# Turning the normalised rows on VectorE in place and storing them from ScalarE's queue

## The chip, the core and the metric

The kernel runs on one core of a Trainium2 chip. The metric is device time in microseconds of one execution, as the median of several runs. The profile comes from one profiled execution on that core.

## The reference

The inputs are q, k, v of shape (4, 8, 576, 64), two weight matrices for a first feed-forward stage and three with a gain for a second. All is float32.

```python
scores = scale * q @ k.T            # per batch and head, D = 64
scores = where(0 <= i - j < 128, scores - slope_h * |i - j|, -1e9)
x = softmax(scores) @ v             # to (2304 tokens, 512)
h = x @ w_in                        # 512 -> 2048
x = (h * clip(h + 3, 0, 6) / 6) @ w_out          # 2048 -> 512
xn = x / sqrt(mean(x * x) + 1e-6) * rms_g
g, val = xn @ w_gate, xn @ w_val    # 512 -> 1536 each
out = (g * sigmoid(g) * val) @ w_out2            # 1536 -> 512
```

## The kernel before

The 2304 tokens are 18 tiles of 128 rows, and three tiles are a block, so there are six blocks, 0 to 5. Every float32 operand of a large product is split into a high and a low float32r part, and each product is three matmuls (high by high, high by low, low by high).

*First feed-forward stage (L683 to L792).* The work runs in parts, in the order of `PARTS`: block 0 with its first 12 slices of the hidden dimension, block 1 with all 16, block 0 with its last 4, then blocks 2 to 5 with 16 each. A part is a loop over slices `m`, and one turn of this loop is called a step here. In a step TensorE computes `product1` (12 matmuls into the one PSUM bank `ps_h`), then pieces of the attention of a later block, then `product2` of the step before (three outputs `o0` to `o2` of three matmuls each). ScalarE and VectorE make the activation of the slice in turn: relu (ACT, L722), multiply (DVE, L723, the last reader of `ps_h`), high part (ACT, L728), low part (DVE, L734). The order of all instructions is written out by hand (`manual_schedule`), and every engine executes its own instructions in that order; the tile framework adds the waits between engines.

*Attention beside it.* For blocks 2 to 5 the attention of one pair of heads takes four steps, and its pieces return every four steps. In the step that begins a group of four (step 0 here), ACT first copies the transposed weights of the pair's first tile out of PSUM (`late`, L709 and L405) and TensorE then transposes those of the second tile into the same PSUM bank, `T` (L400). Step 1 transposes the third tile and splits the next q and k (L310 to L317); step 2 has the score matmuls (L348 or L357); step 3 has the products with v and, at its end, the transposes of the first tile. The last part (block 5) has no attention beside it.

*The rows between the stages (class `Norm`, L505).* When a block has its last `product2`, `Norm` copies the three outputs out of PSUM into three tiles `y` of 128 rows by 512 (L514 to L518). The pool holds three such tiles (`bufs=3`). Then, one tile per step, `square` sums the squares on ACT (L526) and POOL makes the inverse root (L527 to L529); `scale` multiplies the tile by it on DVE (L534); one such step later `back` transposes it with four TensorE transposes into one PSUM bank (L550); and `store`, at the start of the next step, copies this bank to SBUF on ACT (L539) and writes it to DRAM with one DMA of 256 KB from SP's queue (L541). From block 0's own `Norm` on, `back` and `scale` run only in steps 3 and 0 of each four (`go`, L701), and in every step in the last part. So a block's first and third tile are stored at the start of a step 1 and the second at the start of a step 0. Block 1's tiles are scaled and turned during the last part of block 0, in successive steps, and block 0's `Norm` is created, by L614 to L615, right after `back` has turned block 1's last tile; `store` of that tile comes in the next step.

*Second stage (L833 on).* It reads the turned rows of six tiles back as `x2raw` (`Inputs.load`, L634), with the 512 features on partitions in four chunks, scales them by the gain and multiplies them with the weights in seven products per slice (a seven-product scheme for 2x2 blocks). Block 5's `Norm` is finished here: `store` follows the first silu of a group (L945), `scale` the second sum (L946) and `back` the group's end (L957).

Of the kernel before, what the change touches and what calls it, by code (L numbers as in the profile page):

```python
# [10 lines left out]
F32 = mybir.dt.float32  # L11
# [9 lines left out]
P = 128  # L21
B, H, S, D = 4, 8, 576, 64
NT = B * S
NTILE = NT // P
DM = H * D
KC = DM // P
# [6 lines left out]
BLOCKS = [(i, 3) for i in range(0, NTILE, 3)]  # L33
# [28 lines left out]
PAIRS2 = NTILE // 6  # L62
# [11 lines left out]
def fused_kernel(ctx: ExitStack, tc: tile.TileContext, qd, kd, v, w1, w2, rms_g, out):  # L74
# [7 lines left out]
    vec, act, pool, pe, sp = nc.vector, nc.scalar, nc.gpsimd, nc.tensor, nc.sync  # L82
# [6 lines left out]
    dram = ctx.enter_context(tc.tile_pool(name="dram", bufs=1, space=DRAM))  # L89
    ps_out = ctx.enter_context(tc.tile_pool(name="ps_out", bufs=1, space=PSUM))  # L90
    ps_h = ctx.enter_context(tc.tile_pool(name="ps_h", bufs=1, space=PSUM))
    ps_a = ctx.enter_context(tc.tile_pool(name="ps_a", bufs=1, space=PSUM))


    ident = const.tile([P, P], F32, name="ident")
# [57 lines left out]
    class First:  # L153
# [3 lines left out]
        def __init__(self):  # L157
            self.raw = [room(k, [P, 2 * DM], U64, "wraw") for k in range(M1)]
            self.loaded, self.runs, self.tiles = 0, [], []

        def load(self, upto):
            while self.loaded < min(upto, M1):
                sp.dma_start(out=self.raw[self.loaded], in_=w1[self.loaded])
                self.loaded += 1
# [309 lines left out]
            x.scores()  # L474


    x2 = [dram.tile([P, KC, 6 * P], F32, tag=f"x2_{i}", name=f"x2_{i}") for i in range(PAIRS2)]

    def product1(ps, w, xs, n):

# [24 lines left out]
    class Norm:  # L505


        def __init__(self, b, outs, part=None):
            self.b, self.n, self.t = b, len(outs), 0
            self.y, self.ri, self.ps = [], {}, {}  # L510
            for i, o in enumerate(outs):
                y = ypool.tile([P, DM], F32, tag="y", name="y")
                if part:
                    vec.scalar_tensor_tensor(out=y, in0=o, scalar=1.0 / 6.0, in1=part[i], op0=ALU.mult, op1=ALU.add)  # L514
                elif i % 2:
                    act.activation(y, o, AF.Copy, scale=1.0 / 6.0)
                else:
                    vec.tensor_scalar(y, o, 1.0 / 6.0, None, ALU.mult)  # L518
                self.y.append(y)
            self.square(0)  # L520
# [13 lines left out]
                vec.tensor_scalar(self.y[t], self.y[t], self.ri[t], None, ALU.mult)  # L534

        def store(self):
            for k in list(self.ps):
                yt = ypool.tile([P, KC, P], F32, tag="yt", name="yt", bufs=1)
                act.copy(yt, self.ps.pop(k))  # L539
                i = BLOCKS[self.b][0] + k  # L540
                sp.dma_start(out=x2[i // 6][:, :, i % 6 * P : (i % 6 + 1) * P], in_=yt)  # L541

        def back(self):

            k = self.t - 1
            if 0 <= k < self.n:
                tag = "T" if self.b == len(BLOCKS) - 1 else f"S{k % 2}"
                ps = ps_a.tile([P, KC, P], F32, tag=tag, name="ps_x")
                for c in range(KC):
                    pe.transpose(ps[:, c], self.y[k][:, c * P : (c + 1) * P], ident)  # L550
                self.ps[k] = ps
            self.square(self.t + 1)
            self.t += 1
            return self.t <= self.n + 1
# [70 lines left out]
    class Inputs:  # L625
# [5 lines left out]

        def load(self):
            self.x = xpool.tile([P, KC, 6 * P], F32, tag="xs", name="x2raw")
            sp.dma_start(out=self.x, in_=x2[self.s])  # L634

        def block(self, r, c):
            return self.x[:, 2 * c : 2 * c + 2, r * self.n : (r + 1) * self.n]
# [45 lines left out]
    for p, (b, m0, m1) in enumerate(PARTS):  # L683
        n = BLOCKS[b][1]
        last = p == len(PARTS) - 1
        nq = n * P
        if p == 2:
            conv.close()
            ypool = ys.enter_context(tc.tile_pool(name="ypool", bufs=3, **OPEN))
        if last:  # L690
# [3 lines left out]
            ypool = p2.enter_context(tc.tile_pool(name="ypool2", bufs=3, **OPEN))  # L694
# [3 lines left out]
        for m in range(m0, m1):  # L698
# [13 lines left out]
            ps = ps_h.tile([P, 4 * P], F32, tag="h", name="ps_h")  # L712
# [8 lines left out]
            r = gpool.tile([P, 3 * P], F32, tag="t", name="t", bufs=1)  # L721
# [25 lines left out]
            if p == 0:  # L747
                k = m + 1
# [18 lines left out]
            if last:  # L767
# [6 lines left out]
                for x in early:  # L774
                    k = m - EARLY[x.m]
# [20 lines left out]
    n = 3 * P  # L796
# [109 lines left out]
    for m, x in parts.items():  # L906
        i = m - 2
# [32 lines left out]
    for i in range(M2 * PAIRS2):  # L940
        s, m = divmod(i, M2)
# [63 lines left out]
```

## Time and profile before

| what | value |
|---|---|
| time, median of 3 runs | 956.75 us (956.23 to 956.86) |
| span of the profiled execution, first to last instruction | 954.2 us |
| TensorE matmuls busy | 937.7 us, 98% |
| VectorE (DVE) busy | 640.5 us, 67% |
| ScalarE (ACT) busy | 454.2 us, 48% |
| GpSimd (POOL) busy | 186.3 us, 20% |
| DMA, all from SP's queue | 174.09 MB, 52.2% of 16 engines' time |
| TensorE clock granted, mean | 0.995 of full speed |

The page gives no time of the profiled execution besides its span; the median of the runs is 2.55 us longer than it. Instructions that issue DMAs aren't counted as busy: a row of such an instruction, marked SPq, gives the time for which SP was held by it.

### The profile page before, as it was taken

How to read it: one execution, taken by the hardware profiler on the slowest of the kernel's cores; microseconds unless marked ns; L12 is line 12 of the kernel's file. 1: busy time of each engine (PE TensorE's matmuls, PEld its weight loads, DVE VectorE, ACT ScalarE, POOL GpSimd, SP SyncE). 2: the span in 40 equal slices, each digit the busy share in tenths (PEclk: the TensorE clock that was granted, in tenths of full speed). 3: DMA queues.
4: the chain of work that ended last, by engine and by line, in shares of the span. 5: the costliest groups of instructions: out<-in, count | busy, mean ns of one | idle time of the engine just before them, and what ended most of it. 6: DMA issues, size and time to landing. Idle time of an engine off the chain costs nothing.

```text
span 954.2 us, 14654 instructions
## 1 busy us (share of the span) xinstructions
PE 937.7 (98%) x5336; PEld 832.9 (87%) x5336; DVE 640.5 (67%) x1336; ACT 454.2 (48%) x969; POOL 186.3 (20%) x327
## 2 busy tenths in 40 slices
PE   7899999999999999999999999999999999999998
PEld 4587888888888888888899999999999999999996
DVE  5788667555878777877467657777545577545555
ACT  6899566455666655655455453433131323231120
POOL 4333012332223332422124223310000000000000
PEclk8999999999999999999999999999999999999999
DMA  6555401113666555554355757866757555755521
GB/s 231 183 194 194 187 20 51 32 53 117 198 211 203 172 164 174 164 169 130 122 182 210 287 206 293 320 229 234 249 212 281 214 202 199 265 206 211 214 86 67
DMA packets 67432, 175.02 MB, mean 183 GB/s; under 512 B 5024, under 2 KB 41888, under 8 KB 62624
## 3 DMA queue, kind: packets, MB, share of 16 engines
q1 hardware_dynamic: 67360, 174.09, 52.2%
q8 instruction: 42, 0.69, 0.3%
q14 instruction: 30, 0.25, 0.1%
HBM read 130.03 MB, written 44.04 MB: 182 GB/s over the span
## 4 chain that ended last, share of the span: by engine, by line
PE 87%; DVE 6%; ACT 4%; issue 2%; POOL 1%; ACTq 0%; POOLq 0%; DVEq 0%
PE ps_o L497 19%; PE ps_h L484 18%; PE ps_y L892 15%; PE ps_o L845 10%; PE ps_S L845 8%; PE ps_A L845 6%; PE ps_h L845 4%; PE ps_av L418 2%; PE ps_t L400 2%; PE ps_s L357 1%; DVE wx L143 1%; PE ps_s L348 1%; ACT t L386 1%; ACT wx L136 1%; DVE t L371 1%
## 5 line engine op out<-in xcount | busy, mean ns | idle before, releaser
L497 PE MATMUL ps_o<-w,g 128*128 128x512 f32 x864 | 224.0, 402 | 2.1 <-DVE w L147 1.9
L484 PE MATMUL ps_h<-xs,w 128*128 128x384 f32 x1152 | 220.2, 339 | 0.0
L484 PEld LDWEIGHTS ps_h<-xs,w 128*128 128x128 f32 x1152 | 202.4, 188 | 5.8 <-issue 0.2
L497 PEld LDWEIGHTS ps_o<-w,g 128*128 128x128 f32 x864 | 156.2, 188 | 41.1 <-issue 6.3
L892 PE MATMUL ps_y<-wo,g 128*128 128x512 f32 x648 | 150.2, 390 | 0.5 <-DVE g L881 0.5
L892 PEld LDWEIGHTS ps_y<-wo,g 128*128 128x128 f32 x648 | 121.3, 188 | 25.1 <-DVE g L881 0.9
L723 DVE SCALAR_TENSOR_TENSOR t<-t,ps_h 128x384 f32<-128x384 f32 x96 | 53.2, 554 | 98.7 <-ACT t L722 98.6
L722 ACT ACTIVATE t<-ps_h,three 128x384 f32<-128x384 f32 x96 | 55.5, 578 | 84.1 <-PE ps_h L484 80.2
L899 DVE TENSOR_TENSOR y<-y,ps_y 128x512 f32<-128x512 f32 x90 | 61.7, 686 | 35.3 <-PE ps_y L892 35.0
L386 ACT ACTIVATE t<-t,m 128x128 f32<-128x128 f32 (+1 forms) x144 | 61.4, 428 | 29.4 <-DVE t L378 14.2
L728 ACT CAST g<-t 128x384 fp32r<-128x384 f32 x96 | 49.5, 516 | 47.5 <-DVE t L723 46.2
L734 DVE TENSOR_TENSOR g<-t,g 128x384 fp32r<-128x384 f32 x96 | 54.4, 567 | 23.3 <-ACT g L728 23.0
L868 ACT ACTIVATE r<-r 128x384 f32<-128x384 f32 x36 | 19.0, 527 | 105.6 <-DVE r L867 105.6
L845 PE MATMUL ps_o<-S,tw 128*128 128x384 f32 x336 | 66.2, 339 | 0.3 <-DVE t L865 0.3
L388 POOL TENSOR_SCALAR r<-den 128x2 f32<-128x2 f32 x72 | 27.4, 380 | 187.6 <-ACT t L386 186.0
L845 PEld LDWEIGHTS ps_o<-S,tw 128*128 128x128 f32 x336 | 59.3, 188 | 1.4 <-DVE u L856 0.8
L389 POOL TENSOR_TENSOR r<-r,minus 128x2 f32<-128x2 f32 x72 | 56.0, 778 | 6.0
L407 POOL TENSOR_SCALAR_AFFINE_SELECT pt<-pt 128x256 f32<-128x256 f32 x82 | 34.5, 421 | 107.5 <-ACT pt L405 104.5
L853 ACT COPY s<-ps_S 128x384 f32<-128x384 f32 x18 | 8.7, 481 | 86.9 <-PE ps_S L845 86.9
L371 DVE CUSTOM_DVE_ANT_0 t<-ps_s,rel 128x256 f32<-128x256 f32 (+2 forms) x128 | 45.2, 395 | 3.6 <-PE ps_s L357 3.6
L143 DVE SCALAR_TENSOR_TENSOR wx<-wx,wy 128x512 uint32<-128x512 uint32 (+1 forms) x52 | 44.2, 850 | 0.0
L136 ACT ACTIVATE wx<-wraw 128x512 f32<-128x512 f32 (+1 forms) x52 | 42.8, 824 | 0.0
(138 smaller groups left out, 1471.9 us busy)
## 6 DMA issues: line engine op xcount, KB each, us to landing
tw<-t SPq DMA_DIRECT2D x52, 896.0 KB, 6.3
wraw<-w SPq DMA_DIRECT2D x36, 512.0 KB, 4.1
wo<-w SPq DMA_DIRECT2D x18, 1024.0 KB, 4.9
wraw<-w SPq DMA_DIRECT2D x16, 1024.0 KB, 9.1
t<-th SPq DMA_DIRECT2D x12, 896.0 KB, 4.3
t<-tl SPq DMA_DIRECT2D x12, 896.0 KB, 4.3
b<-wx SPq DMA_DIRECT2D x24, 256.0 KB, 2.6
w<-w SPq DMA_DIRECT2D x12, 512.0 KB, 3.0
```

The source lines that it names most:

```text
L143: vec.scalar_tensor_tensor(out=xi, in0=xi, scalar=3, in1=y, op0=ALU.logical_shift_left, op1=ALU.bitwise_or)
L371: vec.tensor_tensor_reduce(out=self.t[:, a, c0:], in0=s[:, c0:], in1=(rel_split if self.i in SPLITS else rel)[:, c0:], scale=2.0 ** (-8.0 ...
L386: act.activation(p, p, AF.Exp, bias=self.m[:, a : a + 1], scale=-1.0, accum_out=self.den[:, a : a + 1])
L389: pool.tensor_tensor(self.r, self.r, minus, ALU.pow)
L484: pe.matmul(ps[:, : n * P], lhsT=w[:, a, c * P : (c + 1) * P], rhs=xs[c][:, b, : n * P], start=(k == 0), stop=(k == 3 * KC - 1),)
L497: pe.matmul(o, lhsT=g[:, a, i * P : (i + 1) * P], rhs=w[:, b], start=(m == first and a == 0 and b == 0), stop=(m == last and a == 1),)
L722: act.activation(r[:, :nq], ps[:, :nq], AF.Relu, bias=three)
L723: vec.scalar_tensor_tensor(out=r[:, :nq], in0=r[:, :nq], scalar=6.0, in1=ps[:, :nq], op0=ALU.min, op1=ALU.mult)
L734: vec.tensor_sub(g[:, 1, :nq], r[:, :nq], f32(g[:, 0, :nq]))
L845: pe.matmul(ps, lhsT=w[a][:, k, c * P : (c + 1) * P], rhs=x[:, b, c], start=(start and j == 0), stop=(j == 5), skip_group_check=True,)
L892: pe.matmul(ps, lhsT=gs[i + k][:, a, t // 3, t % 3 * P : (t % 3 + 1) * P], rhs=wo[i + k][:, b], start=(k == 0 and a == 0 and b == 0), stop ...
L899: vec.tensor_add(acc[t], acc[t], ps)
```

## The change

`back` no longer uses TensorE: it transposes the tile in place with one VectorE instruction, which turns each 32x32 block where it stands. `store` no longer copies anything: it issues four DMAs from ScalarE's own queue, one for each 32 partitions, and the DMA's destination puts the blocks where they belong. In such a quarter, partition r holds for each of 16 groups f of features the 32 tokens of feature 32 f + r, so one DMA has 32 x 16 = 512 runs of 32 floats, 128 bytes each. The DRAM tile `x2` becomes a plain matrix of 512 features by 768 tokens, and `load` reads it by rows of 768 floats into the same SBUF layout as before. The tile `y` is now read by the DMAs.

```diff
-    x2 = [dram.tile([P, KC, 6 * P], F32, tag=f"x2_{i}", name=f"x2_{i}") for i in range(PAIRS2)]
+    x2 = [dram.tile([DM, 6 * P], F32, tag=f"x2_{i}", name=f"x2_{i}") for i in range(PAIRS2)]
...
         def store(self):
-            for k in list(self.ps):
-                yt = ypool.tile([P, KC, P], F32, tag="yt", name="yt", bufs=1)
-                act.copy(yt, self.ps.pop(k))
-                i = BLOCKS[self.b][0] + k
-                sp.dma_start(out=x2[i // 6][:, :, i % 6 * P : (i % 6 + 1) * P], in_=yt)
+            for k in list(self.turned):
+                yt, i = self.turned.pop(k), BLOCKS[self.b][0] + k
+                for a in range(4):
+                    c0 = i % 6 * P + a * 32
+                    act.dma_start(
+                        out=x2[i // 6][:, c0 : c0 + 32].rearrange("(f r) s -> r f s", r=32),
+                        in_=yt[a * 32 : (a + 1) * 32].rearrange("r (f s) -> r f s", s=32),
+                    )
 
         def back(self):
 
             k = self.t - 1
             if 0 <= k < self.n:
-                tag = "T" if self.b == len(BLOCKS) - 1 else f"S{k % 2}"
-                ps = ps_a.tile([P, KC, P], F32, tag=tag, name="ps_x")
-                for c in range(KC):
-                    pe.transpose(ps[:, c], self.y[k][:, c * P : (c + 1) * P], ident)
-                self.ps[k] = ps
+                self.turned[k] = self.y[k]
+                vec.transpose(self.y[k], self.y[k])
             self.square(self.t + 1)
...
         def load(self):
             self.x = xpool.tile([P, KC, 6 * P], F32, tag="xs", name="x2raw")
-            sp.dma_start(out=self.x, in_=x2[self.s])
+            sp.dma_start(out=self.x, in_=x2[self.s].rearrange("(c p) n -> p c n", p=P))
```

## Rows read from the trace of the kernel before

**Rows 1.** The page, part 1: busy us, share of the span, instructions.

```profile
PE 937.7 (98%) x5336; PEld 832.9 (87%) x5336; DVE 640.5 (67%) x1336; ACT 454.2 (48%) x969; POOL 186.3 (20%) x327
```

**Rows 2.** Two stretches: length, busy us of PE, PEld, DVE, ACT, POOL, clock, DMA.

```profile
190.00:220.00 30.00, 30.00 (x186) 26.15 (x183) 16.17 (x49) 14.80 (x40) 9.09 (x21) 1.00 0.18 52
560.00:600.00 40.00, 39.73 (x214) 36.82 (x213) 25.79 (x36) 17.50 (x30) 11.62 (x13) 1.00 0.78 284
```

**Rows 3.** Chain of waits by windows: start us, us; first and last of 17.

```profile
207.36 0.44 PE ps_x L550 x4
...
588.11 0.44 PE ps_x L550 x4
```

**Rows 4.** Timeline, block 0's second tile (step 0): start us, us.

```profile
255.80 0.48 DVE L534 TENSOR_SCALAR y<-y,ri 128x512 f32<-128x512 f32 x1
256.46 0.38 ACT L405 COPY pt<-ps_t 128x256 f32<-128x256 f32 x1
258.08 0.38 PE L400 MATMUL ps_t<-ident,t 128*128 128x128 f32 x2
```

**Rows 5.** Timeline, block 0's first tile and the steps behind it.

```profile
239.44 0.48 DVE L534 TENSOR_SCALAR y<-y,ri 128x512 f32<-128x512 f32 x1
242.00 0.58 ACT L722 ACTIVATE t<-ps_h,three 128x384 f32<-128x384 f32 x1 [1.40 <-PE ps_h L484]
244.81 0.69 DVE L317 TENSOR_TENSOR ks<-kraw,ks 128x512 fp32r<-128x512 f32 x1
246.29 0.96 PE L348 MATMUL ps_s<-ks,qs 64*128 64x128 f32 x12
```

**Rows 6.** Lines 541 and 256 on SP, min/median/max ns; landing of 541's DMA.

```profile
L541 SPq DMA_DIRECT2D x<-yt x18: 512/548/621, 210.4 to 592.8; - x18
DMA to landing us min/median/max: 2.5/3.0/9.4
...
L256 SPq DMA_DIRECT2D t<-th x12: 319/320/383, 489.5 to 627.3; - x12
```

**Rows 7.** Timeline, block 2's second tile (block 3's has the same order).

```profile
340.22 0.58 ACT L539 COPY yt<-ps_x 128x512 f32<-128x512 f32 x1
340.68 0.38 ACT L405 COPY pt<-ps_t 128x256 f32<-128x256 f32 x1
```

**Rows 8.** Timeline, block 1's tiles and the start of block 0's `Norm`.

```profile
209.82 0.59 ACT L539 COPY yt<-ps_x 128x512 f32<-128x512 f32 x1
210.30 0.59 ACT L722 ACTIVATE t<-ps_h,three 128x384 f32<-128x384 f32 x1
213.38 0.48 DVE L534 TENSOR_SCALAR y<-y,ri 128x512 f32<-128x512 f32 x1
216.25 0.38 PE L400 MATMUL ps_t<-ident,t 128*128 128x128 f32 x2
218.73 1.88 DVE L514 SCALAR_TENSOR_TENSOR y<-ps_o,part 128x512 f32<-128x512 f32 x3
219.49 0.64 ACT L526 ACTIVATE junk<-y 128x512 f32<-128x512 f32 x1 [1.27 <-DVE y L514]
221.23 2.31 PE L497 MATMUL ps_o<-w,g 128*128 128x512 f32 x9
```

**Rows 9.** Timeline, block 4's tiles in the last part.

```profile
475.76 3.17 DVE L643 TENSOR_SCALAR x2raw<-x2raw,g_sb 128x768 f32<-128x768 f32 x4
480.02 2.35 PE L484 MATMUL ps_h<-xs,w 128*128 128x384 f32 x12
488.93 1.40 PE L484 MATMUL ps_h<-xs,w 128*128 128x384 f32 x7
```

**Rows 10.** The page, part 5: busy us, mean ns, idle before.

```profile
L723 DVE SCALAR_TENSOR_TENSOR t<-t,ps_h 128x384 f32<-128x384 f32 x96 | 53.2, 554 | 98.7 <-ACT t L722 98.6
L728 ACT CAST g<-t 128x384 fp32r<-128x384 f32 x96 | 49.5, 516 | 47.5 <-DVE t L723 46.2
L734 DVE TENSOR_TENSOR g<-t,g 128x384 fp32r<-128x384 f32 x96 | 54.4, 567 | 23.3 <-ACT g L728 23.0
```

More of the change, by code (lines that the diff above doesn't have):

```diff
@@ L509, in __init__ @@
             self.b, self.n, self.t = b, len(outs), 0
-            self.y, self.ri, self.ps = [], {}, {}
+            self.y, self.ri, self.turned = [], {}, {}
             for i, o in enumerate(outs):
```

## The prediction

> **What bounds the kernel now.** I read the page's busy shares first, then the chain of waits, then single stretches in order of time. TensorE is busy for 937.7 of 954.2 us [rows 1]; in the stretch of the first three stores it has no gap at all (30.00 of 30.00 us) [rows 2]. So a microsecond that leaves TensorE's order is worth a microsecond, and one in which TensorE has to wait costs one. The other engines matter only where TensorE waits for them, so what counts is how late ScalarE (ACT) and VectorE (DVE) may be in each single step. The span is 954.2 us and the median of the runs 956.75 us; I sum against the span and add the 2.55 us between them, as launch and end, unchanged.
>
> **What goes.** The four PE transposes of one tile stand on the chain with 0.44 us [rows 3]. The chain, window by window, holds 17 of the 18 groups (the other lies beside a longer chain of VectorE and ScalarE): 17 x 0.44 = 7.5 us is the most that TensorE can give back. The copy out of PSUM (0.58 us of ACT) and one DMA issue on SP go too. Nothing waits for that issue, except twice a next copy, so SP's relief is worth nothing.
>
> **What comes, per tile.** (1) One VectorE transpose of 128x512 f32, behind which all later DVE work of the step queues. The trace has none. The nearest rows are the in-place multiply of the same tile, 0.48 us [rows 4], and a two-input operation of the same size, 0.69 us [rows 5]. These are my bounds; I take 0.60, between them, since the transpose has one input like the first and its rate isn't shown. (2) Four DMA issues in ACT's own order. They wait for the transpose, and ACT executes in order, so the copy of attention weights (L405), the relu (L722) and the casts of the next step queue behind them. The trace has no issue on ACT; on SP the DMA with the same number of runs (512, then of 512 B, now of 128 B) takes 0.512 to 0.621 us, and the shortest issue of any kind 0.319 [rows 6]. I take 0.60 each with the gap to the next: 2.4 us per tile; the low end is 4 x 0.36 = 1.4, and for the high end I take 1.0 each, about twice SP's median, for four in a row.
>
> The Trainium skill ("Perfetto Trace Analysis", section DMA Instruction — HWDGE) says that the issuing sequencer is held from the end of its semaphore wait through a wait for the one descriptor generator until the descriptors are made. SP's rows agree in size; by that rule ACT would hold for all four.
>
> **Where it decides.** The steps of the first product have a rhythm of four. "Stored" is the start of the step after `back()`. I compare the start of the same instruction before and after; 0.44 us saved is inside each difference.
>
> *The second tile of blocks 0, 2, 3 (step 0 of four).* Here the copy of `late` weights follows the store on ACT, and TensorE's next transposes need the PSUM bank that this copy empties. In block 0 DVE's multiply ends at 256.28; transpose to 256.88; issues to 259.28; the 0.38 us copy to 259.66. TensorE's transposes started at 258.08 and now start at 259.7 [rows 4]: 1.6 us lost. In blocks 2 and 3 ACT first waits for a DVE conversion that now stands behind the new transpose; before, the copy of weights began 0.46 us after the PSUM copy and TensorE was already waiting for it [rows 7]. So +0.60 + 2.4 - 0.46 = 2.5 us lost each. Together 6.6 us.
>
> *The first and third tile of these blocks (step 1).* Multiply to 239.92, transpose to 240.52, issues to 242.92; the relu that began at 242.00 is 0.92 late. The chain relu, cast, split of k passes this on: the last DVE split ends at 246.4 and not 245.5, against a score matmul at 246.29 [rows 5]: 0.1 us lost. The two other first tiles come out near zero; for all three 0.4 us lost. For the third tiles, with no multiply ahead of the transpose, there is just room: 0.3 us gained each, 0.9 together.
>
> *Block 1.* Its first store comes where the copy began, 209.82; issues to 212.22, and the relu at 210.30 is 1.92 late. All DVE work behind it is, too: multiply to 215.78, transpose to 216.38, issues to 218.78, copy to 219.16, and TensorE's transposes slip from 216.25 to 219.2, by 2.95 us. Then a wait that was not there: block 0's three y tiles take the three buffers of tag `y`, and the third still holds block 1's last tile. Before, its PE transpose had read it. Now a DMA must, and `store()` issues that DMA one step later. Block 0's first write moves from 218.73 to 218.73 + 2.95 + 0.60 = 222.28; it lasts 0.63, the square on ACT some 0.8 to 223.7, the four issues to 226.1, the last of them starting at 225.5; landing takes a median of 3.0 us [rows 6], to 228.5; then the third write, to 229.2. TensorE's third output of the next second product needs that PSUM bank: the product would begin at 221.23 + 2.95 - 0.44 = 223.7 and reach it at 225.2. It waits 4.0 us and ends at 229.9, not 223.54 [rows 8]. Lost: 6.4 us.
>
> *Block 4 (no attention beside it).* DVE's four scalings begin at 475.76 and last 3.17; 0.60 ahead of them puts their end at 479.5, and after the 0.55 us of L723 the bank of `ps_h` is free at 480.1, where the first product began at 480.02 [rows 9, 10]: no gain. The next round is a ring: cast, subtract, multiply and transpose, 0.52 + 0.57 + 0.48 + 0.60, to 482.3; issues to 484.7; relu and L723, 0.58 + 0.55, to 485.8, with gaps 486.0, and only then may the first product start again. The last round has no multiply: 486.0 + 1.69 + 2.4 + 1.13 = 491.2 against 488.93 [rows 9, 10]. Lost: 2.3 us.
>
> *Block 5 (second product).* ACT is busy 17.50 of 40 us [rows 2]; it sits between long matmul groups, and the 2.4 us are hidden. Gain: 3 x 0.44 = 1.3 us. If that room were gone, as much as 2 us each would be lost.
>
> The load of x2 now reads 3 KB runs and not 12 KB; it is issued a step or more ahead, and I cost it at nothing. TensorE's clock shows 1.00, its higher level, in both stretches [rows 2]; waits of 2 to 4 us don't change that in my sum.
>
> **Sum:** -6.6 - 0.4 + 0.9 - 6.4 - 2.3 + 1.3 = -13.5, so 13.5 us lost. The span becomes 967.7, and with the 2.55 us outside it 970.2.
>
> The Trainium skill ("DMA: Bandwidth & Descriptors", Specifications) asks for at least 512 B per run for line rate and says that below it DMA reads, modifies and writes. No row here has data runs of 128 B. By it the landing in block 1 would be longer than 3.0 us: at twice that, 3 us more, 973.2.
>
> **Rivals.**
> *A cheap issue.* An issue on ACT costs what the simplest one costs on SP, 0.32 plus the gap, 1.4 us per tile [rows 6]. Then step 0 loses 0.7 in block 0 and 1.5 each in blocks 2 and 3; block 1 loses 3.7 (its slip is 0.9, the wait for the landing 3.3); block 4 loses 0.4; the first and third tiles gain 0.4 each (2.6), block 5 1.3. Net 3.9 lost: 960.7. Against it: the issue with the same count of runs never took under 0.512.
> *A crowded queue.* The four issues in a row can't hand over 2,048 runs as fast as SP hands over 512, and each takes 1.0 us. The 1.6 us more per tile pass on in about 12 of the 18 tiles, 19 us, and the landing is 3 us later: about 992. For it: landings of this DMA of up to 9.4 us [rows 6]. Against it: the median of 3.0.
> *Faster.* ACT gets past the issues nearly free, because the real cost is on the queue and not on the engine. From 0.60 to 0.36 per issue the loss falls by 9.6 us, so it turns into a gain below some 0.26 us each. At 0.1 the step-0 tiles lose about 1.5 in all, block 1 still loses 2.0 for its buffer, the rest gains 5: 955.2. If the buffer's wait were hidden too, 7.5 us: 949.2. Against it: no issue in the trace is below 0.319.
> *Block 1's buffer doesn't wait that long* (landing 2.0, or a free buffer): up to 4.0 less, 966.2. It lies within my range.
>
> **How the numbers follow.** Forecast 0.57 (its own range 964 to 978), cheap issue 0.18 (958 to 963), crowded queue 0.11, faster or even 0.14. What this kernel's measurement can tell from no change is about 0.2%, 1.9 us. Of the last case 0.09 is faster and 0.05 within that; of the cheap issue 0.02 comes within it as well. So faster 0.09, same 0.07, slower 0.84. The range is 956.5 to 984: it leaves out what is faster and the upper part of the crowded queue.
>
> **What would show it.** Four issues of 0.5 to 0.6 us in a row on ACT after each transpose; TensorE's transposes at step 0 (L400) idle until ACT's copy L405, some 2 us in three blocks and more in block 1; the third write of L514 waiting for a DMA near 223 us, and a gap of about 4 us in the second product there; TensorE's busy time down by about 10 us while the span grows. The forecast is wrong if the issues on ACT take under 0.3 us, if relu starts stay where they were, or if L514 doesn't wait.

## The result, and the profile after

The changed kernel takes 970.13 us (median; 966.86 to 973.09) against 956.49 us, a ratio of 1.0145, 95% interval 1.0130 to 1.0161. The forecast was 970.2. A second measurement of the same kernel, further down, gave 969.05 us and 1.0139 [1.0125, 1.0153]. The profiled execution is the quickest of the first four: 966.86 us, span 965.0, which is 10.8 us longer than the span before.

First the page of the changed kernel, parts 1, 3 and 4 (q1 is SP's queue, q10 ScalarE's):

```profile
PE 934.9 (97%) x5264; PEld 825.5 (86%) x5264; DVE 652.4 (68%) x1354; ACT 444.1 (46%) x951; POOL 183.5 (19%) x327
...
q1 hardware_dynamic: 59008, 169.37, 49.8%
q10 hardware_dynamic: 38016, 4.72, 3.2%
...
PE 73%; DVE 12%; ACT 7%; issue 3%; DMA 2%; ACTq 1%; POOL 1%; SPq 0%; POOLq 0%; DVEq 0%
```

TensorE has 72 instructions less than in [rows 1] and yet a longer span: 30.1 us of it are now idle, where it was 16.5. Its share of the chain that ended last is 73%, against 87% before.

The tile `y` in the changed kernel (min/median/max ns) answers to [rows 6]:

```profile
L541 ACTq DMA_DIRECT2D x<-y x72: 309/517/1874, 209.3 to 604.2; - x72
...
L551 DVE STREAM_TRANSPOSE y<-y x18: 698/704/708, 208.5 to 600.0; 128x512 f32<-128x512 f32 x18
...
DMA to landing us min/median/max: 1.8/2.3/12.9
```

So the transpose costs 0.70 us and an issue 0.52 us, and the data land in 2.3 us in the median, although the runs have 128 bytes. The windows of the changed kernel (columns as in [rows 2]):

```profile
190.00:220.00 30.00, 27.50 (x163) 23.57 (x160) 15.98 (x48) 13.19 (x37) 8.85 (x21) 0.96 0.28 65
218.50:222.00 3.50, 3.50 (x13) 2.84 (x12) 3.28 (x7) 1.32 (x4) 1.13 (x2) 0.65 0.94 302
258.00:266.00 8.00, 5.34 (x29) 4.48 (x29) 5.92 (x15) 3.56 (x8) 0.87 (x2) 1.00 0.93 269
266.00:270.00 4.00, 4.00 (x23) 3.67 (x22) 2.62 (x5) 0.94 (x3) 0.40 (x1) 1.00 0.76 145
```

The stretch of block 1's stores had no gap; now 2.5 of 30 us are idle. Behind that gap the clock shows 0.65: part of this stretch ran at half speed (1.2 GHz).

The timeline of the changed kernel, the first issue of block 1's first tile, block 1's last two tiles, block 0's second tile and block 4's first, answers to [rows 4, 8, 9]:

```profile
209.28 0.35 ACTq L541 DMA_DIRECT2D x<-y  x1
...
214.85 0.70 DVE L551 STREAM_TRANSPOSE y<-y 128x512 f32<-128x512 f32 x1
215.59 1.97 ACTq L541 DMA_DIRECT2D x<-y  x4
217.65 0.37 ACT L405 COPY pt<-ps_t 128x256 f32<-128x256 f32 x1 [4.17 <-issue]
218.07 0.69 PE L400 MATMUL ps_t<-ident,t 128*128 128x128 f32 x2 [2.50 <-ACT pt L405]
218.41 3.51 PE L497 MATMUL ps_o<-w,g 128*128 128x512 f32 x9
220.77 1.25 DVE L514 SCALAR_TENSOR_TENSOR y<-ps_o,part 128x512 f32<-128x512 f32 x2
221.46 0.63 ACT L526 ACTIVATE junk<-y 128x512 f32<-128x512 f32 x1 [1.82 <-DVE y L514]
221.47 0.86 ACTq L541 DMA_DIRECT2D x<-y  x2
222.36 1.07 ACTq L541 DMA_DIRECT2D x<-y  x2
...
225.12 0.69 DVE L514 SCALAR_TENSOR_TENSOR y<-ps_o,part 128x512 f32<-128x512 f32 x1 [3.10 <-DMA x<-y]
225.87 0.50 PE L497 MATMUL ps_o<-w,g 128*128 128x512 f32 x1 [0.25 <-DVE y L514]
...
260.04 0.70 DVE L551 STREAM_TRANSPOSE y<-y 128x512 f32<-128x512 f32 x1
260.77 2.40 ACTq L541 DMA_DIRECT2D x<-y  x4
263.22 0.37 ACT L405 COPY pt<-ps_t 128x256 f32<-128x256 f32 x1 [3.99 <-DMA x<-y]
263.64 0.44 PE L400 MATMUL ps_t<-ident,t 128*128 128x128 f32 x2 [2.66 <-ACT pt L405]
...
485.02 1.97 ACTq L541 DMA_DIRECT2D x<-y  x4
487.09 0.58 ACT L722 ACTIVATE t<-ps_h,three 128x384 f32<-128x384 f32 x1 [3.08 <-issue]
489.05 2.37 PE L484 MATMUL ps_h<-xs,w 128*128 128x384 f32 x12 [1.14 <-DVE t L723]
```

The order is the predicted one: transpose, four issues in 1.97 to 2.40 us, ScalarE's next instruction right behind them, and TensorE 2.50 and 2.66 us idle at L400 (2.15 and 2.30 in blocks 2 and 3) and 1.14 us at L484 in block 4.

### The profile page after: what moved, and what is told of

Its sections match the earlier page's. It is cut to its first block, busy times and chain, and to the rows that moved or that the text cites. A ratio compares the mean times of both kernels' runs of the same rounds, so it can differ in the third digit from the quotient of the medians.

```text
span 965.0 us, 14564 instructions
## 1 busy us (share of the span) xinstructions
PE 934.9 (97%) x5264; PEld 825.5 (86%) x5264; DVE 652.4 (68%) x1354; ACT 444.1 (46%) x951; POOL 183.5 (19%) x327
## 3 DMA queue, kind: packets, MB, share of 16 engines
q1 hardware_dynamic: 59008, 169.37, 49.8%
q10 hardware_dynamic: 38016, 4.72, 3.2%
## 4 chain that ended last, share of the span: by engine, by line
PE 73%; DVE 12%; ACT 7%; issue 3%; DMA 2%; ACTq 1%; POOL 1%; SPq 0%; POOLq 0%; DVEq 0%
PE ps_y L892 15%; PE ps_o L497 13%; PE ps_h L484 13%; PE ps_o L845 10%; PE ps_S L845 8%; PE ps_A L845 6%; PE ps_h L845 4%; DVE t L723 2%; PE ps_av L418 2%; ACT t L722 2%; DVE wx L143 2%; ACT t L386 1%; PE ps_t L400 1%; DMA wraw<-w 1%; DVE t L371 1%
## 5 line engine op out<-in xcount | busy, mean ns | idle before, releaser
L497 PE MATMUL ps_o<-w,g 128*128 128x512 f32 x864 | 225.4, 404 | 2.3 <-DVE w L147 1.9
L484 PE MATMUL ps_h<-xs,w 128*128 128x384 f32 x1152 | 220.2, 339 | 3.5 <-DVE t L723 3.3
L484 PEld LDWEIGHTS ps_h<-xs,w 128*128 128x128 f32 x1152 | 202.3, 188 | 13.1 <-DVE t L723 7.2
L497 PEld LDWEIGHTS ps_o<-w,g 128*128 128x128 f32 x864 | 157.1, 189 | 41.7 <-issue 6.1
L728 ACT CAST g<-t 128x384 fp32r<-128x384 f32 x96 | 49.3, 514 | 51.8 <-DVE t L723 50.2
L400 PE MATMUL ps_t<-ident,t 128*128 128x128 f32 x190 | 35.4, 290 | 16.9 <-ACT pt L405 11.0
L400 PEld LDWEIGHTS ps_t<-ident,t 128*128 128x128 f32 x190 | 24.7, 146 | 28.0 <-ACT pt L405 15.5
```

Source lines behind the costliest of these rows:

```text
L400: pe.transpose(self.ps[:, a, c], self.t[:, a, c * P : (c + 1) * P], ident)
L484: pe.matmul(ps[:, : n * P], lhsT=w[:, a, c * P : (c + 1) * P], rhs=xs[c][:, b, : n * P], start=(k == 0), stop=(k == 3 * KC - 1),)
L497: pe.matmul(o, lhsT=g[:, a, i * P : (i + 1) * P], rhs=w[:, b], start=(m == first and a == 0 and b == 0), stop=(m == last and a == 1),)
```

## The experiments

All are the changed kernel with one edit, unless told otherwise; ratios are against the kernel before, measured beside each. "Blocks unplaced" means that the 32x32 blocks stay where the transpose left them, so that the DMA has runs of 512 bytes and the output is another; without the transpose the output is another too.

| edit | us, median (range) | ratio, 95% interval |
|---|---|---|
| changed kernel again | 969.05 (967.82 to 971.75) | 1.0139 [1.0125, 1.0153] |
| DMAs from SP's queue | 952.84 (952.18 to 953.41) | 0.9966 [0.9952, 0.9979] |
| copy of weights ahead of the store | 967.78 (966.04 to 969.23) | 1.0121 [1.0108, 1.0135] |
| one DMA on ScalarE, blocks unplaced | 953.09 (951.95 to 954.19) | 0.9969 [0.9957, 0.9980] |
| four DMAs of 128 runs, blocks unplaced | 966.76 (965.33 to 968.71) | 1.0113 [1.0099, 1.0127] |
| four y buffers | 968.78 (968.12 to 972.20) | 1.0143 [1.0126, 1.0161] |
| four y buffers, store behind the cast | 961.22 (960.54 to 961.93) | 1.0054 [1.0041, 1.0066] |
| SP's queue, four y buffers | 951.50 (950.82 to 951.79) | 0.9951 [0.9938, 0.9963] |
| SP's queue, no transpose | 948.79 (948.22 to 949.01) | 0.9923 [0.9909, 0.9936] |
| SP, four buffers, transpose a step later | 949.72 (949.39 to 950.33) | 0.9934 [0.9921, 0.9946] |
| kernel before, its DMA from ScalarE | 958.35 (958.01 to 960.05) | 1.0027 [1.0018, 1.0036] |
| changed kernel, TensorE's waits filled | 967.61 (967.15 to 967.95) | 1.0122 [1.0105, 1.0139] |

**The queue.**

```diff
-                    act.dma_start(
+                    sp.dma_start(
```

> The same change, but the four DMAs of a tile are issued from SyncE's queue (SP), which executes nothing else that TensorE waits for. Theory (ScalarE is held by its own issues): the late copies of weights and late relus go, only the 0.70 us of the transpose on VectorE is left as a delay. The 7.5 us that TensorE gave back then show nearly whole: the three step-0 stalls and block 1's stall of 2.7 us at 216 us disappear, block 4 loses under 1 us; 949 to 954 us. Rival (the runs of 128 bytes and their landing are what costs): the time stays within 2 us of the changed kernel, 965 to 971, and the third write of L514 still waits for a DMA. Rival (VectorE's transpose is the delay): between the two, 958 to 963.

16 us of difference for the queue alone, with the same runs of 128 bytes and the same transposes. The engine that is held by the issues is the cause; the size of the runs is not. One stall stays in block 1; TensorE also waits 0.39 and 0.56 us at L400 in blocks 2 and 3, and 1.14 us at L484 in block 4. Timeline with SP's queue, blocks 1 and 2:

```profile
221.82 0.69 DVE L514 SCALAR_TENSOR_TENSOR y<-ps_o,part 128x512 f32<-128x512 f32 x1 [2.45 <-DMA x<-y]
222.57 0.97 PE L497 MATMUL ps_o<-w,g 128*128 128x512 f32 x3 [1.37 <-DVE y L514]
...
339.43 0.44 PE L400 MATMUL ps_t<-ident,t 128*128 128x128 f32 x2 [0.39 <-ACT pt L405]
```

**How many issues, or how many runs.** One DMA per tile of 512 runs of 512 bytes; and four DMAs of 128 such runs each:

```diff
-                for a in range(4): ...                       # 4 x 512 runs of 128 B
+                act.dma_start(out=x2[...][:, c0 : c0 + P].rearrange("(c p) s -> p c s", p=P), in_=...)
...
+                for a in range(4):                           # 4 x 128 runs of 512 B
+                    act.dma_start(out=x2[...][a * P : (a + 1) * P, c0 : c0 + P].rearrange("(c p) s -> p c s", p=32), in_=...)
```

> The changed kernel with one DMA per tile from ScalarE's queue in place of four, 512 runs of 512 bytes as in the kernel before; the blocks stay where VectorE's transpose left them, so the turning is done only within blocks of 32x32 and the output is another. Theory (ScalarE's held time is what costs): one issue holds it for 0.4 to 0.6 us and not 2.0, so 1.4 to 1.6 us less per tile; all step-0 stalls shrink to some 0.8 us or less: 952 to 958 us. Rival (VectorE's 0.70 us and the new buffer wait): 962 to 968.

> The changed kernel with four DMAs per tile from ScalarE's queue, but with runs of 512 bytes: each has 32 partitions x 4 runs, 128 runs and not 512; the blocks stay where VectorE's transpose left them, so the output is another. If ScalarE's held time goes with the number of runs, an issue falls from 0.52 to some 0.35 us or below and the time to 957 to 962 us. If it goes with the number of DMAs, the issues stay at 0.5 us and the time at 966 to 971.

With one DMA the loss is gone, on ScalarE's queue as before. Timeline of block 0's second tile with one DMA: one short issue, the copy behind it, and no wait at L400.

```profile
257.35 0.37 ACTq L540 DMA_DIRECT2D x<-y  x1
257.76 0.37 ACT L405 COPY pt<-ps_t 128x256 f32<-128x256 f32 x1 [1.94 <-DVE y L550]
...
258.19 0.44 PE L400 MATMUL ps_t<-ident,t 128*128 128x128 f32 x2
```

With four DMAs of a quarter of the runs the time stays at 966.8, and the issue falls only from 517 to 456 ns; neither expected case fits exactly, the one by the number of DMAs nearly:

```profile
L541 ACTq DMA_DIRECT2D x<-y x72: 309/456/1032, 210.0 to 605.9; - x72
```

**ScalarE's order.** First only the copy of weights goes ahead of the store; then, with four y buffers, the whole store goes behind the cast L728.

```diff
-            for x in norms:
-                x.store()
             for x in late:
                 x.weights()
+            for x in norms:
+                x.store()
```

> The changed kernel with the late copy of weights (L405) ahead of the store in ScalarE's order at the start of a step; all else as it is, ScalarE still issues four DMAs per tile. Theory: TensorE at step 0 waits for the PSUM bank which that copy empties; with the copy first the stalls at L400 of blocks 0 to 3 go (2.8, 2.3, 2.3 and in block 1 2.7 us, 10 in all), and the issues then delay only the relu, which has some room in step 0: 957 to 961 us. Rival (the relu of the same step is as late as the copy and its delay reaches TensorE one step later): 964 to 970 us, with the stalls moved from L400 to L484 or the scores.

The rival was right: 967.78. Timeline with the copy first, block 0's second tile: the copy is early, now the relu is behind the issues, and TensorE waits at the next first product.

```profile
260.67 0.37 ACT L405 COPY pt<-ps_t 128x256 f32<-128x256 f32 x1
...
262.31 3.27 ACTq L541 DMA_DIRECT2D x<-y  x4
...
265.68 0.58 ACT L722 ACTIVATE t<-ps_h,three 128x384 f32<-128x384 f32 x1 [4.65 <-PE ps_o L497]
...
266.90 1.50 PE L484 MATMUL ps_h<-xs,w 128*128 128x384 f32 x4 [2.09 <-DVE t L723]
```

```diff
-            for x in norms:
-                x.store()
...
             act.copy(g[:, 0, :nq], r[:, :nq])
+            for x in norms:
+                x.store()
```

> As with four y buffers, and the store moved in ScalarE's order from the start of a step to behind the cast of the step's high part (L728), where ScalarE has just ended its part of the chain relu, multiply, cast, split; all four DMAs stay on ScalarE's queue. Theory (ScalarE has some 50% of idle time, and it is the place in its order that costs): the issues lie in its slack, the stalls at L400 go, and the time comes to 951 to 957 us. Rival (2 us on ScalarE pass on to TensorE wherever they stand, as they did when only the copy of weights was put ahead of them): 961 to 968 us.

961.22 us: near the edge of the rival's range. The place matters for more than half of the loss (7.8 us of the 13.1 that the changed kernel beside it loses; the fourth buffer alone brings nothing, as the next run shows), but at this place, too, ScalarE had no room for all four issues. Timeline behind block 0's third tile: the issues now delay the split of k, and the scores wait (they started without a wait in [rows 5]).

```profile
263.05 2.24 ACTq L541 DMA_DIRECT2D x<-y  x4
...
265.34 0.62 ACT L310 ACTIVATE qs<-qraw,qscale 128x384 fp32r<-128x384 f32 x1 [1.78 <-issue]
...
267.27 0.96 PE L348 MATMUL ps_s<-ks,qs 64*128 64x128 f32 x12 [0.42 <-DVE ks L317]
```

**Block 1's buffer.**

```diff
-                y = ypool.tile([P, DM], F32, tag="y", name="y")
+                y = ypool.tile([P, DM], F32, tag="y", name="y", bufs=3 if b == len(BLOCKS) - 1 or b == 4 else 4)
```

> The changed kernel with four y buffers in place of three while blocks 0 to 3 are worked on, so that block 0's third write of L514 need not wait for the DMAs of block 1's last tile. By the prediction that wait costs TensorE 4.0 us: 4 us less than the changed kernel beside it. By the profile of the changed kernel the product behind it ends only some 0.3 to 1.3 us later for it, since the relu and the bank of the step before are late anyway: 0 to 1.5 us less.

> The changed kernel once more, unaltered, on the chip of the three runs beside it, so that they have it as their measure. Its first four times lay between 966.9 and 973.1 us with clocks from 0.993 down to 0.984: again 966 to 973 here, and the time should rise as the granted clock falls, since a wait of TensorE of 2 to 3 us was followed by a stretch of half the clock in the profile.

No difference that can be measured: 968.78 against 969.05 beside it, with the wait of L514 gone. With SP's queue the same edit is worth 1.3 us by the medians, 951.50 against 952.84, and the ranges of their runs lie apart. The two were measured on different chips, on which the kernel before differs by 0.2 us; by the starts of the same matmuls in the two profiles block 1 gains 1.7 us.

> The four DMAs from SP's queue, and four y buffers. From SP alone the time was 952.8 us, and its profile has one stall left in block 1, of 1.4 to 1.8 us, where the third write of L514 waits 2.5 us for a DMA. Theory: it goes, 951.0 to 951.9 us. Rival (the time comes back at the next late instruction): 952.4 to 953.2.

**The clock.** In the second measurement of the changed kernel the time rose with a falling clock only in part: 967.82 and 969.44 at 0.995, 968.66 and 971.75 at 0.989. Windows and two timeline rows of its profile (971.75 us), behind the stalls of blocks 0 and 2. The first profile has a clock of 1.00 there: at 266 us above, and behind block 2's stall in the window that follows.

```profile
266.00:270.00 4.00, 4.00 (x15) 3.57 (x14) 3.10 (x7) 0.84 (x2) 0.54 (x2) 0.57 0.53 102
350.50:354.50 4.00, 3.88 (x12) 3.15 (x13) 3.39 (x7) 2.03 (x5) 1.69 (x4) 0.62 0.90 278
```

The first profile, block 2:

```profile
348.00:352.00 4.00, 4.00 (x21) 3.64 (x22) 3.50 (x8) 1.87 (x4) 1.68 (x4) 1.00 0.93 285
```

And the second profile's timeline:

```profile
350.62 0.44 PE L400 MATMUL ps_t<-ident,t 128*128 128x128 f32 x2 [2.13 <-ACT pt L405]
...
350.81 3.62 PE L497 MATMUL ps_o<-w,g 128*128 128x512 f32 x9
```

Nine matmuls that take 2.31 us in [rows 8] take 3.62: 1.3 us lost behind a wait of 2.13. In all, this profile has half clock behind the stalls of all four blocks (0 to 3), the first one behind block 1's alone, and its span is 4.9 us longer. In blocks 2 and 3 the stalls are as long as in the first (2.13 and 2.30 us against 2.15 and 2.30), and the first product behind them starts another 1.3 and 1.5 us late; in block 0 the stall itself is longer (3.39 us against 2.66), since one issue took 1.47 us. The test fills the wait with matmuls whose results are unused:

```diff
+            fill = late and any(x.turned for x in norms)   # ahead of the store
...
             product1(ps, W1.w_in(m), xs, n)
+            if fill:
+                spare = ps_a.tile([P, KC, P], F32, tag="S0", name="spare")
+                for _ in range(8):
+                    pe.matmul(spare[:, 0], lhsT=ident, rhs=ident, start=True, stop=True)
```

> The changed kernel with eight matmuls of 128x128 (some 1.5 us, results unused) on TensorE where it waits at step 0 of a second tile, between the first product and the transposes L400; ScalarE and VectorE do the same as in the changed kernel, so TensorE's order is only filled up where it stood. Theory (a wait of 2 to 3 us is sometimes followed by a stretch of half the clock, which is lost in addition and makes the times spread): no such stretch behind L400, the times close to the best of the changed kernel or below, 964 to 967 us, the granted clock 0.994 or above in all runs. Rival (the clock's falls have another cause, and the spread with them): 968 to 972 us as the changed kernel, the same spread.

The spread of four executions falls from 3.9 us (6.2 in the first four) to 0.8, and the clock shows 1.00 in the windows that had 0.57 and 0.62, though 0.33 to 0.91 us of the waits at L400 are left:

```profile
266.00:270.00 4.00, 4.00 (x23) 3.68 (x22) 2.75 (x6) 1.10 (x3) 0.23 (x1) 1.00 0.67 165
350.50:354.50 4.00, 4.00 (x23) 3.68 (x22) 2.66 (x5) 0.63 (x2) 0.15 (x1) 1.00 0.88 227
```

The median missed its expected 964 to 967, though, and isn't clearly below the unfilled one (the intervals overlap). One reason is in the timeline of the filled kernel: without the fall of the clock in block 1, TensorE reaches the occupied bank sooner and waits there instead.

```profile
225.74 0.69 DVE L514 SCALAR_TENSOR_TENSOR y<-ps_o,part 128x512 f32<-128x512 f32 x1 [3.28 <-DMA x<-y]
226.49 0.96 PE L497 MATMUL ps_o<-w,g 128*128 128x512 f32 x3 [1.95 <-DVE y L514]
```

**The transpose's price, and a version that beats both.** With SP's queue, once without the transpose; then with it, four buffers, and the transpose moved out of `back` to the next step's `store`, ahead of the DMAs:

```diff
             for k in list(self.turned):
                 yt, i = self.turned.pop(k), BLOCKS[self.b][0] + k
+                vec.transpose(yt, yt)
...
                 self.turned[k] = self.y[k]
-                vec.transpose(self.y[k], self.y[k])
```

> The four DMAs from SP's queue (three y buffers) and no transpose at all: the rows are written unturned, so the output is another. Beside the run with SP alone (952.8 us) the difference is the price of 18 VectorE transposes of 0.70 us. By that run's profile TensorE loses for them 0.5 us in each of blocks 2 and 3 and 0.9 in block 4, and a little of the wait in block 1: 949.5 to 951.5 us. Rival (VectorE's idle time hides them): 952.3 to 953.3.

> SP's queue and four y buffers, and the VectorE transpose moved from the end of a step to the start of the next, ahead of the multiply L723, where VectorE waits for the relu. Theory (the 0.70 us delays the conversions that ScalarE and TensorE wait for at step 0, and there is room before the multiply): the 0.5 us of blocks 2 and 3 and the 0.9 of block 4 go, 949.3 to 950.6 us. Rival (it delays the multiply and by it the bank of ps_h): 951 to 953 us.

Without any transpose 948.79, 4.1 us less than with SP's queue alone and a little below the expected 949.5: VectorE's 0.70 us isn't hidden where it stood. By the starts of the same matmuls in the two profiles, 1.7 us of it is block 1's wait for the buffer, which is gone without the transpose, 0.6 each lies in blocks 2 and 3, and 1.1 in block 4. Moved, and with the fourth buffer, it costs 0.9 us: 949.72, 1.8 us less than with four buffers and the transpose in `back` (951.50), and 6.3 us below the kernel before (956.00 beside it). In its timeline, block 0's second tile, VectorE does its conversions of weights (L143 to L140) ahead of the transpose, L400 doesn't wait, and the tile is turned just before the multiply. Its page shows 7.0 us less of TensorE than [rows 1].

```profile
255.42 0.38 PE L400 MATMUL ps_t<-ident,t 128*128 128x128 f32 x2
255.50 0.68 DVE L539 STREAM_TRANSPOSE y<-y 128x512 f32<-128x512 f32 x1
...
256.21 2.05 SPq L542 DMA_DIRECT2D x<-y  x4
256.28 0.56 DVE L723 SCALAR_TENSOR_TENSOR t<-t,ps_h 128x384 f32<-128x384 f32 x1
```

Its page, part 1:

```profile
PE 930.7 (98%) x5264; PEld 825.3 (87%) x5264; DVE 651.9 (69%) x1354; ACT 444.0 (47%) x951; POOL 185.1 (20%) x327
```

**The queue in the kernel before.**

```diff
-                sp.dma_start(out=x2[i // 6][:, :, i % 6 * P : (i % 6 + 1) * P], in_=yt)
+                act.dma_start(out=x2[i // 6][:, :, i % 6 * P : (i % 6 + 1) * P], in_=yt)
```

> The kernel before, with TensorE's transposes, the copy out of PSUM and its single DMA per tile, but this DMA issued from ScalarE's queue: the queue alone. Theory (held time): an issue of 0.37 to 0.55 us behind the copy, which makes the late copy of weights at step 0 in blocks 2 and 3 late by as much and touches little else: 956.5 to 959 us. Rival (a DMA on ScalarE's queue is bad in itself, whatever its number): 962 us or more.

958.35, as expected: one issue more on ScalarE, 2.4 us. The queue is not bad in itself. Its issue, with the number of runs and bytes of the single DMA above, takes 0.52 us and not 0.37:

```profile
L541 ACTq DMA_DIRECT2D x<-yt x18: 520/521/587, 210.5 to 594.8; - x18
```

## Why the prediction was right, and where it was not

Its mechanism is shown. ScalarE is held by its own issues: without three of the four, or without all, the loss is gone (953.1 and 952.8), and with as many issues of fewer runs it stays. L405 starts 0.05 us after the end of the four issues at 260.77. The Trainium skill's rule on the held sequencer ("Perfetto Trace Analysis", DMA Instruction — HWDGE), that it is free only once the descriptors are made, agrees with these rows.

The sum was closer than its terms. I compare starts of the same instruction, after minus before, at the borders of the terms; the profiled execution lost 10.8 us of span, and the borders leave 0.1 over.

| term | predicted loss | in the profile | what was off |
|---|---|---|---|
| block 1 | 6.4 | 3.2 | the buffer's wait: 4.0 predicted, 0.25 found |
| blocks 0, 2, 3 | 6.1 | 5.3 | step 0 alone: 6.6 predicted, 2.4 + 1.8 + 1.8 found |
| block 4 | 2.3 | 2.7 | predicted without gain or loss ahead of the first ring; 0.85 was lost there |
| rest of the last part | 0 | 0.3 | |
| block 5 | -1.3 | -0.6 | half of the gain |

*The step that failed most* is "the third write ... to 229.2 ... It waits 4.0 us". I put the four issues behind the square on ScalarE, at 223.7. They began at 221.47, beside the square that began at 221.46: here an issue waited for the data that it needs, and not for the end of the instruction ahead of it. And the write began 1.7 us after the last issue ended, where I took 3.0 from the last issue's start at 225.5. So it ended at 225.8, and TensorE waited 0.25 us. What block 1 lost instead is the stall of 2.50 at L400, which makes L400 1.8 us late (218.07 for 216.25) and not 2.95, in part because the first tile's issues also began earlier (209.28, where I took 209.82), and 1.2 us of half clock (3.51 for 2.31). Where less else is late, TensorE does wait longer for the buffer: 1.37 us with SP's queue, 1.95 with the waits filled.

*The second* is "waits of 2 to 4 us don't change that in my sum". They did: in some executions a stretch of half clock follows a stall, in others none does behind a stall of the same length (block 2: a clock of 1.00 behind 2.15 us in one profile, 0.62 behind 2.13 in the other). The profiled execution, with one such stretch, is 3.3 us below the median, and the spread goes when the waits are filled. So that 970.2 was met within 0.1 us is luck: a wait was overrated by 3.75 us and the clock left out, and the two errors nearly made up for each other. The second profile shows how the clock can add up to that; how much of each unprofiled time is clock isn't shown, and with the waits filled the median fell by only 1.4 us, within the noise. The Trainium skill ("TensorE: Matmul & The Clock Gate", HAM oscillation — how this bites in real kernels) has the rule: a wait for data can throttle TensorE's clock, and the work behind it starts cold. The clock of 1.00 behind the filled waits agrees.

*Sizes.* The transpose took 0.70 us, just above my upper bound of 0.69, the two-input operation. Four issues took 1.96 to 2.54 us in blocks 0 to 4, mostly 1.97 and not 2.4, as the first of a set is short (0.31 to 0.35); block 5 has sets of 3.62 and 3.09. The rival of the crowded queue isn't borne out in the landing, 2.3 us against 3.0 in [rows 6]; only the DMA engines' time per MB is longer (q10: 3.2% for 4.72 MB, q1: 49.8% for 169.37 MB, 2.3 times as much), and TensorE felt a landing only through block 1's buffer. So the landing gives no sign of the 973.2 that I worked out from the Trainium skill's 512 bytes ("DMA: Bandwidth & Descriptors", Specifications). Of the signs, TensorE's busy time fell by 2.8 us and not by 10: in the last version, without a slow stretch, it falls by 7.0, near the 7.5 that I gave as the most, and in the changed kernel slow matmuls count longer (L497 225.4 us in all against 224.0), which explains a part. The gap of 4 us didn't come; the others showed.

*The rivals.* "Faster" and "cheap issue" fell with the 0.52 us. The 949.2 that I gave for issues that cost nothing and a hidden buffer is nearly what the last version brings (949.72), which has the issues on SP, a fourth buffer and the transpose moved; the issues on SP alone bring 952.84.

## What to carry to other kernels

A DMA issue is an instruction in its engine's order: count issues times half a microsecond, and put them on a queue for which no one waits; on an engine that feeds the bound one, moving them in its order won back nothing clear of the noise at one place and 7.8 us at another, and a stall stayed at both. Work taken off the bound engine pays when its new engine idles at that very place in its order. And when TensorE stalls for a few microseconds, add to the sum what a lower clock may cost behind it, here 1.2 to 1.5 us in some executions.

## What the runs showed of the hardware, unexpected

- An issue on ScalarE runs beside the compute instruction ahead of it (221.47 beside 221.46), while the compute behind it waits for it.
- An issue's time doesn't go with its runs: 0.37 and 0.52 us for a single DMA of 512 runs of 512 bytes written to two layouts of the destination, 0.46 in the median for 128 runs in a row of four. What sets it stays open, as do single issues of up to 1.9 us on ScalarE.
- A stall of 2.1 us (block 2) was followed by a clock of 0.62 in one execution and of 1.00 in another of the same program.
